# Lightning attention and a locality-gated expert layer on one core: the first expert tile turned outside TensorE, gate chances computed in earlier steps, one group of slot products, and another order of the first pair's weight transfers

## The chip, the core and the metric

The kernel runs on one core of a Trainium2 chip. The metric is device time in microseconds (us); smaller is better. One execution was also taken by the hardware profiler. The engines are named as in the profile: PE is TensorE (PEld its weight loads), DVE is VectorE, ACT is ScalarE, POOL is GpSimd, SP the engine that issues most of the DMAs.

## The reference

Attention: for 4 sequences of 768 tokens and 8 heads of 64, a decayed linear attention in blocks, with a running state per head. Its output, written as x with 512 values per token, goes to an expert layer with 8 experts:

```python
logits = np.einsum('bsd,de->bse', x, w_gate)
local_gate = 1.0 / (1.0 + np.exp(-np.einsum('bsd,de->bse', x, w_local).squeeze(-1)))
...
        fresh_e = int(np.argmax(logits[b, s]))
        if s == 0 or local_gate[b, s] < 0.5:
            e = fresh_e
        else:
            e = prev_e if prev_e >= 0 else fresh_e
        prev_e = e
...
        p /= p.sum() + 1e-09
        h = np.maximum(x[b, s] @ w1[e], 0.0)
        out[b, s] = p[e] * (h @ w2[e])
```

So each token has one expert, the fresh one or that of the token before it; a token's output is scaled by the chance p[e] of its expert.

## The kernel before, in words

**Attention.** The work is cut into 24 steps s (0 to 23), one for each 128-token chunk c (6) of each sequence b (4), in the order c outer, b inner. A step issues, on PE: the scores of step s+1 (`scores`, two PSUM tiles ps0 and ps1; steps in the list WIDE use 8 matmuls over 128 columns, L200, the others 16 smaller ones, L208), the part that comes from the state (`from_state`, L235), the part from the masked scores (`mix`, L248), the state update (`update`, L262; not in the last chunk) and four transpositions that turn rows of the step before (`rows_of`, L272). DVE masks the scores (L212, two operations) and adds the state (L265). ACT copies the attention output from the PSUM pair po0, po1 into xc (L251), the turned rows from pk1 into xn (L277), and decays the state (L239). po0, po1 and pk1 exist once, so the next step's L235 and L272 wait until these copies are done. POOL prepares qd and kd (L177, L180), three buffers each. xn goes to the DRAM tensor x_dram: ACT's queue issues these DMAs, in the last steps SP's.

**Routing beside attention.** After every four steps, `gates` and `logits` compute the gate logits of four row tiles of 128 tokens (there are 24). A table `extras` places the routing work at points (s, 0), in the middle of step s, and (s, 1), at its end. For the first 12 row tiles (PARTS 0 and 1) it finds experts (`fresh_experts`, `along_sequences`, `experts_of`), ranks (`ranks`), tiles and slots (`first_tiles`, `tokens_to_first_tiles`), and the chances (`chances`). `brought` multiplies a hit mask by five columns of `parts`: two for the token's number, three for its chance, split into three bf16 pieces. `masks` makes one-hot rows (`lane`), and `by_slots` multiplies both on PE (L619): this gives, for each slot of an expert tile, the token to gather (gidx) and its gate.

**Experts.** Five tiles of 128 tokens (KA = 5) come from the first 12 row tiles. A tile's rows are gathered from x_dram by an indirect DMA on POOL (`collect`, called by `ahead`), must be turned (features on the partitions), then `hidden` (L731) and `output` (L737) run on PE. Tile 0 is turned on PE by `first_turned` (L712) with one DVE copy (L713). All others are turned by `flipped`, a DVE transposition that works inside 32x32 blocks (L717), and `moved`, which puts the blocks in place by sixteen small ACT copies (L724, four for each k). After the five single tiles follow pairs of tiles of one expert (`pair`), computed with seven products for eight (L957, L962) from sums and differences of weights (`sums_1`, `sums_2`, on DVE, L935 to L938). Beside the first pairs run tiles of half size for what remains of an expert (`hooks_of_halves`: L1086, L1096, L1118).

**Weights.** There are three weight buffers (w1t and w2t, 0 to 2), 2 MB for each layer. `weights_of(g, i, layers)` issues the load of tile g's expert into buffer i on SP's queue. SP works through its queue in order and waits, at each load, until the buffer is free. G2 is the number of the first half-size tile; its weights go to buffer 2, whose first-layer half is also the room of `val` in the second `brought`.

**Order.** PE, DVE, SP and POOL run in the written order in the attention and single-tile phase. ACT is not in that list there: a scheduler places ACT's instructions. In the pair phase (from L1180) ACT is in written order as well, and POOL is not.

```python
    with tc.manual_schedule(engines={PE, DVE, SP, POOL}):
```

Of the kernel before, what the change touches and what calls it, by code (L numbers as in the profile page):

```python
# [38 lines left out]
PARTS = [(0, 8), (8, NA), (NA, NT)]  # L39
LOADS = 6  # L40
QUARTERS = [16, 17, 18, 19]
WIDE = [3, 4, 5, 6]
WARM = 10
KA = -(-(NA * P - E * (P - 1)) // P)

# [19 lines left out]
def kernel(  # L65
# [313 lines left out]
    def hot_of(i):  # L379
        lo, hi = PARTS[i]  # L380
        return hots[lo // NA][:, :, lo % NA:lo % NA + hi - lo]
# [81 lines left out]
        nc.vector.tensor_tensor(lane, countb.unsqueeze(1).broadcast_to([P, hi - lo, P]),  # L463
                                place[:, 0, lo:hi].unsqueeze(2).broadcast_to([P, hi - lo, P]), ALU.is_equal)

    def chances(i):

        lo, hi = PARTS[i]
        n = hi - lo
        if i == 2:  # L470
            room = act.tile([P, DM], F32, name="room", bufs=1)
        else:
            room = att.tile([P, DM], F32, name="kd", bufs=3)
        prob = room[:, :n * E].rearrange("p (n e) -> p n e", e=E)
        den, pick = (room[:, k:k + n] for k in (n * E, n * (E + 1)))
        nc.vector.tensor_tensor(prob, lt[:, lo:hi, :E], nows["mx", i].unsqueeze(2).broadcast_to([P, n, E]), ALU.subtract)
        nc.scalar.activation(prob, prob, ACT.Exp)
        nc.vector.tensor_reduce(den, prob, axis=AX.X, op=ALU.add)
        nc.vector.tensor_scalar(den, den, 1e-9, None, ALU.add)
        nc.vector.reciprocal(den, den)  # L480
        nc.vector.tensor_tensor(prob, prob, hot_of(i).rearrange("p e t -> p t e"), ALU.mult)
        nc.vector.tensor_reduce(pick, prob, axis=AX.X, op=ALU.add)
        nc.vector.tensor_tensor(pick, pick, den, ALU.mult)
        for k in range(2, 5):
            nc.vector.tensor_copy(parts[:, lo:hi, k], pick)
            if k < 4:
                nc.vector.tensor_tensor(pick, pick, parts[:, lo:hi, k], ALU.subtract)

    def span(i):
        return ((0, KA), (KA, G))[i]  # L490
# [216 lines left out]
    def ahead(g, i):  # L707
        collect(xgt[i], *at(g))

    def first_turned():  # L710
        for d in range(DT):
            nc.tensor.transpose(pr[:, P * d:P * d + P], xgt[0][:, P * d:P * d + P], ident)  # L712
        nc.vector.tensor_copy(xtt[0].rearrange("p d i -> p (d i)"), pr)  # L713

    def flipped(xq, xg):

        nc.vector.transpose(xq, xg)  # L717
# [48 lines left out]
    def number(k, n):  # L766
# [4 lines left out]
    extras = {  # L771
        (6, 1): constants_2, (7, 1): constants_3, (8, 1): constants_4, (9, 1): constants_5, (10, 1): constants_6,
        (9, 0): lambda: fresh_experts(0), (10, 0): lambda: along_sequences(0), (11, 0): lambda: experts_of(0),
        (12, 0): lambda: ranks(0), (13, 0): lambda: fresh_experts(1), (14, 0): lambda: (along_sequences(1), masks(0)),
        (15, 0): lambda: experts_of(1), (16, 0): lambda: ranks(1), (17, 0): first_tiles,
        (18, 0): tokens_to_first_tiles, (19, 0): lambda: (brought(0, (0, 1)), masks(1)),
        (19, 1): lambda: by_slots(0, (0, 1)), (20, 0): lambda: (ahead(0, 0), ahead(1, 1), rows_out(0)),
        (20, 1): lambda: chances(0), (21, 0): lambda: chances(1), (22, 0): lambda: brought(0, (2, 3, 4)),
    }

    def extra_work(s, k):
# [3 lines left out]
    with tc.manual_schedule(engines={PE, DVE, SP, POOL}):  # L785

        warm = pg.tile([P, A, P], F32, name="pk0")
        for _ in range(WARM):
            nc.tensor.matmul(warm[:, 0], lhsT=ident, rhs=ident, start=True, stop=True)
        masks_of_lam()  # L790
        nc.gpsimd.memset(wgt, 0.0)
        constants_1()

        for s in range(LOADS - 1):
            inp[s] = load.tile([P, 4, DM], F32, name="inp")
        for s, half in ((0, 0), (1, 0), (0, 1), (1, 1), *((s, half) for s in range(2, LOADS - 1) for half in range(2))):
            nc.sync.dma_start(out=inp[s][:, 2 * half:2 * half + 2], in_=qkv[s][:, 2 * half:2 * half + 2])
        for s in range(3):
            prepare(s)
        scores(0)  # L800
        nc.sync.dma_start(out=wgt[:, :, :E + 1], in_=wg)
        for s in range(NS):
            if s + LOADS - 1 < NS:
                loaded(s + LOADS - 1)
            if s + 3 < NS and s != 1:
                prepare(s + 3)
            if s in QUARTERS:
                j = QUARTERS.index(s)
                nc.sync.dma_start(out=w1t[0][:, j], in_=w1_src(0)[:, j])
            if s == NS - 4:  # L810
                nc.sync.dma_start(out=w2t[0], in_=w2_src(0))
                weights(0)
            if s == NS - 1:
# [12 lines left out]
            mix(s)  # L826
            if s == 0:
                update(0)
                query_powers(0)
            if s in (1, 2, 3, 4):  # L830
                scores(s + 1)
            if s == 1:
                query_powers(1)
                prepare(4)
                rows_of(0)
            if s:
                update(s)
            if s + 1 == NS:
                first_turned()
            if s > 1:  # L840
                rows_of(s - 1)
            extra_work(s, 1)
        x_ctx.close()
        act = ctx.enter_context(tc.tile_pool(name="act", bufs=2))
        w1t.append(act.tile([P, DT, F], F32, name="w1_2", bufs=1))
        w2t.append(act.tile([P, FT, DM], F32, name="w2_2", bufs=1))
        pools.append(act)

        pys.extend(pg.tile([P, DM], F32, name=f"pk{i}") for i in range(2))
        hq.update({(f, 1): act.tile([P, FT // 2, P], F32, name=f"h{f}1", bufs=1) for f in range(2)})  # L850
        xgh = act.tile([P, DM], F32, name="xgh", bufs=1)
        yt = act.tile([P, 2, DM], F32, name="y", bufs=1)
        xps = [act.tile([P, DT, P], F32, name=f"xp{i}", bufs=1) for i in range(3)]
        xs = act.tile([P, 3, DT // 2, P], F32, name="xs", bufs=1)
        s1 = act.tile([P, 3, DT // 2, F // 2], F32, name="s1", bufs=1)
        yl = s1[:, 0]
        s2 = act.tile([P, 3, FT // 2, DM // 2], F32, name="s2", bufs=1)
        hs = act.tile([P, 4, FT // 2, P], F32, name="hsum", bufs=1)
        part = act.tile([P, 3, FT // 2, P], F32, name="part", bufs=1)
        rest = act.tile([P, DM // 2], F32, name="rest", bufs=1)  # L860

        def finished(g):
            output(g % 2, g % 2)
            written(g, g % 2)

        def hiddens(g):
            hidden(g % 2, g % 2, 0)
            hidden(g % 2, g % 2, 1)


        xqs.extend((xlast, rt.tile([P, DM], F32, name="lg")))
        ahead(2, 0)
        xq = hq[1, 0].rearrange("p f i -> p (f i)")
        flipped(xq, xgt[1])
        ahead(3, 1)
        moved(xtt[1], xq, (0, 1))
        hidden(0, 0, 0)
        rows_of(NS - 1)
        weights(1)
        gates(NC - 1)  # L880
        moved(xtt[1], xq, (2, 3))
        hidden(0, 0, 1)
        by_slots(0, (2, 3, 4))
        logits(NC - 1)
        fresh_experts(2)
        flipped(xqs[1], xgt[0])
        ahead(4, 0)
        moved(xtt[0], xqs[1])
        finished(0)
        weights(2)  # L890
        along_sequences(2)
        flipped(xqs[0], xgt[1])
        hiddens(1)
        moved(xtt[1], xqs[0])
        experts_of(2)
        chances(2)
        flipped(xqs[1], xgt[0])
        finished(1)
        weights(3)
        ranks(2)  # L900
        masks(2)
        other_tiles()
        tokens_to_other_tiles()
        hiddens(2)
        moved(xtt[0], xqs[1])
        output(0, 0)
        weights(4)
        brought(1, (0, 1, 2, 3, 4))
        written(2, 0)
        hiddens(3)  # L910
        weights_of(KA, w_of(0), (1,))
        output(1, 1, range(FT // 2))
        by_slots(1, (0, 1, 2, 3, 4))
        weights_of(G2, 2)
        output(1, 1, range(FT // 2, FT))
        written(3, 1)

# [262 lines left out]
    with tc.manual_schedule(engines={PE, DVE, SP, ACTE}):  # L1180
        more, fulls, halves = (number(k, n) for k, n in enumerate((PMAX - PMIN + 1, E + 1, FIRST_SMALL + 1)))
        weights_of(KA, w_of(0), (2,))
        both_halves()
        pair_ahead(0)
        rows_out(1)
# [147 lines left out]
```

## Time and profile before

| | |
|---|---|
| time, median of 3 runs | 453.33 us (451.4 to 454.59) |
| profiled execution, its own time | 451.95 us |
| its span | 450.1 us, granted TensorE clock 0.994 |
| PE busy | 431.8 us (96%) |
| DVE, ACT, POOL busy | 278.9 us (62%), 201.7 us (45%), 109.3 us (24%) |
| DMA | 124.85 MB, mean 277 GB/s |
| 32x128 block copies on ACT (L724) | 295 ns each |

The profiled execution's time is its span and some 2 us around it. In lines of the profile, `L731 PE MATMUL ps<-xt,w` means: line 731 of the kernel, on PE, a matmul into ps from xt and w. A square bracket after an instruction holds the idle time of its engine just before it and what ended it. In a table of waits the numbers are the total in us, how many times, and the longest. The attention phase reaches to about 102 us, the single tiles to 178 us, the pairs and half-size tiles from there on.

### The profile page before, as it was taken

The page shows a single profiled execution, that of the slowest core. Times are in us where ns is not written, and L with a number is a line of the kernel's source. Part 1 is how long each engine was busy: PE and PEld are TensorE (multiplying, and loading weights), DVE is VectorE, ACT ScalarE, POOL GpSimd, SP SyncE. Part 2 cuts the span into 40 slices and gives each one's busy share as a digit, 9 for nine tenths or more (in the row PEclk, how much of TensorE's full clock was granted, in tenths as well). Part 3 has the DMA queues.
Part 4 walks back from the last instruction along what each step waited for, and adds up shares of the span by engine and source line. Part 5 has one row for each costly group of instructions (what it writes and reads, how often), then busy time and mean ns, then how long its engine had stood idle before and what let it go on. Part 6 is the DMA issues. An engine that isn't in the chain of part 4 may idle for free.

```text
span 450.1 us, 10497 instructions
## 1 busy us (share of the span) xinstructions
PE 431.8 (96%) x4186; PEld 358.5 (80%) x4186; DVE 278.9 (62%) x562; ACT 201.7 (45%) x594; POOL 109.3 (24%) x120
## 2 busy tenths in 40 slices
PE   6999998899999999799999999999999999999993
PEld 5877786778667776788685999677799999898982
DVE  5547776871429949576463796100487888878661
ACT  2356665547454104543524448441445455556110
POOL 4476565231100041203220400110102011020101
PEclk9999999999999999999999999999999999999997
DMA  8999999979899899999994499997163838380101
GB/s 269 409 420 411 327 305 317 360 260 367 310 375 353 287 400 379 358 387 399 388 345 176 145 404 375 352 348 286 43 211 93 309 103 284 147 280 6 52 3 51
DMA packets 42575, 124.85 MB, mean 277 GB/s; under 512 B 3148, under 2 KB 3148, under 8 KB 40592
## 3 DMA queue, kind: packets, MB, share of 16 engines
q1 hardware_dynamic: 34976, 104.62, 63.4%
q0 software_dynamic: 4368, 13.90, 9.0%
q10 hardware_dynamic: 3168, 5.51, 3.2%
q8 instruction: 37, 0.61, 0.5%
q14 instruction: 26, 0.21, 0.1%
HBM read 124.02 MB, written 12.91 MB: 304 GB/s over the span
## 4 chain that ended last, share of the span: by engine, by line
PE 77%; DMA 12%; issue 6%; DVE 4%; POOLq 0%; POOL 0%
PE ps L731 11%; PE pk L962 11%; PE pk L737 11%; PE ps L957 10%; DMA out_dram<-y,sidxp 6%; PE po L248 5%; DMA w<-in_w_dram 5%; PE po L957 5%; PE pl L962 4%; PE ps L208 3%; PE pk L272 3%; PE pk L262 2%; PE po L235 2%; PE pr L1118 2%; PE pr L1096 2%
## 5 line engine op out<-in xcount | busy, mean ns | idle before, releaser
L731 PEld LDWEIGHTS ps<-xt,w 128*128 128x128 f32 x512 | 58.2, 192 | 3.0 <-issue 2.3
L731 PE MATMUL ps<-xt,w 128*128 128x128 f32 x512 | 59.1, 276 | 0.3 <-DVE xt L713 0.3
L737 PE MATMUL pk<-w,h 128*128 128x512 f32 x128 | 56.5, 593 | 0.0
L737 PEld LDWEIGHTS pk<-w,h 128*128 128x128 f32 x128 | 23.6, 190 | 26.3 <-issue 25.6
L703 POOL DMA_INDIRECT xg<-x_dram,gidx x25 | 25.8, 1032 | 59.2 <-DVE lg L717 27.7
L746 POOL DMA_INDIRECT out_dram<-y,sidx x14 | 14.0, 1001 | 105.8 <-DVE y L763 46.5
L212 DVE TENSOR_TENSOR sm<-ps,mask 128x512 f32<-128x512 f32 x46 | 29.7, 685 | 15.1 <-PE ps L208 7.6
L724 ACT COPY xp<-xlast 32x128 f32<-32x128 f32 x128 | 37.8, 295 | 1.7
L733 ACT ACTIVATE h<-ps 128x512 f32<-128x512 f32 x16 | 9.6, 597 | 57.6 <-PE ps L731 57.6
L724 ACT COPY xp<-lg 32x128 f32<-32x128 f32 x112 | 33.0, 295 | 2.6
L763 DVE TENSOR_SCALAR y<-pk,gate 128x512 f32<-128x512 f32 x8 | 5.9, 743 | 42.1 <-PE pk L737 30.4
L957 PEld LDWEIGHTS ps<-xp,w 128*128 128x128 f32 x256 | 30.5, 192 | 1.7 <-issue 1.3
L177 POOL TENSOR_TENSOR qd<-inp,lamq 128x512 f32<-128x512 f32 x20 | 25.6, 1278 | 24.9 <-PE po L235 11.4
L957 PE MATMUL ps<-xp,w 128*128 128x128 f32 x256 | 31.3, 275 | 0.0
L957 PE MATMUL ps<-xs,s 128*128 128x128 f32 x256 | 31.2, 275 | 0.0
L962 PE MATMUL pk<-w,h 128*128 128x256 f32 x128 | 30.5, 381 | 0.0
L962 PE MATMUL pk<-s,hsum 128*128 128x256 f32 x128 | 30.3, 380 | 0.0
L248 PE MATMUL po<-sm,inp 128*64 128x128 f32 x384 | 27.7, 280 | 2.5 <-DVE sm L212 1.6
L957 PEld LDWEIGHTS ps<-xs,s 128*128 128x128 f32 x256 | 29.9, 192 | 0.0
L248 PEld LDWEIGHTS po<-sm,inp 128*64 128x64 f32 x384 | 20.9, 136 | 9.5 <-issue 6.6
L962 PEld LDWEIGHTS pk<-s,hsum 128*128 128x128 f32 x128 | 23.9, 190 | 3.3 <-DVE s L1045 0.2
L962 PEld LDWEIGHTS pk<-w,h 128*128 128x128 f32 x128 | 23.5, 190 | 3.4 <-issue 0.6
(280 smaller groups left out, 792.0 us busy)
## 6 DMA issues: line engine op xcount, KB each, us to landing
w<-in_w_dram SPq DMA_DIRECT2D x43, 2048.0 KB, 11.4
inp<-in_qkv_dram SPq DMA_DIRECT2D x15, 1024.0 KB, 8.0
x_dram<-xn ACTq DMA_DIRECT2D x21, 256.0 KB, 7.2
inp<-in_qkv_dram SPq DMA_DIRECT2D x10, 512.0 KB, 7.7
inp<-in_qkv_dram SPq DMA_DIRECT2D x4, 768.0 KB, 6.3
w<-in_w_dram SPq DMA_DIRECT2D x4, 512.0 KB, 9.8
x_dram<-xn SPq DMA_DIRECT2D x2, 256.0 KB, 8.1
xg<-x_dram,gidx POOLq DMA_INDIRECT x25, 6.8
```

Of the source, the lines that this page charges most:

```text
L177: nc.gpsimd.tensor_tensor(qd, x[:, 0].rearrange("p (a i) -> p a i", i=P), lamq, ALU.mult)
L208: nc.tensor.matmul(ps[u][half, a, first:], lhsT=kt[rows, a, half], rhs=qt[rows, a, first:], start=True, stop=True, skip_group_check=True)
L212: nc.vector.tensor_tensor(sm[:, u], ps[u], mask[:, u], ALU.mult)
L248: nc.tensor.matmul(head(a, u), lhsT=vn[:, a, u], rhs=sm[:, u, a], start=(not c and a < 2), stop=True, skip_group_check=True)
L272: nc.tensor.transpose(px[:, P * a:P * a + P], xc[:, a, ORDER[s][0]], ident)
L703: nc.gpsimd.indirect_dma_start(out=xg, out_offset=None, in_=x_dram[:n, :], in_offset=bass.IndirectOffsetOnAxis(ap=gidx[i][:, j:j + 1], axi ...
L724: copy(xt[QP * j:QP * j + QP, :, QP * k:QP * k + QP], blocks[QP * k:QP * k + QP, :, j])
L731: nc.tensor.matmul(ph[:, j], lhsT=w1t[w][:, d, P * f:P * f + P], rhs=xtt[i][:, d], start=(d == 0), stop=(d == DT - 1))
L737: nc.tensor.matmul(pys[i], lhsT=hq[f // 4, i][:, f % 4], rhs=w2t[w][:, f], start=(f == 0), stop=(f == FT - 1))
L746: apart(nc.gpsimd.indirect_dma_start(out=out, out_offset=bass.IndirectOffsetOnAxis(ap=sidx[i][:, j:j + 1], axis=0), in_=y, in_offset=None, ...
L957: nc.tensor.matmul(to[:, m], lhsT=a[:, k, P * m:P * m + P], rhs=b[:, k], start=(new and not m and not k), stop=(k == 1), skip_group_check= ...
L962: nc.tensor.matmul(to, lhsT=a[:, f], rhs=b[:, f], start=(new and not f), stop=(f == FT // 2 - 1), skip_group_check=True)
```

## The change

It has five parts.

1. Step 6 leaves WIDE: its scores use the 16 smaller matmuls.
2. `chances` for PARTS 0 and 1 is split into three pieces and moved from (20, 1) and (21, 0) to the ends of steps 11, 12, 13 and 15, 16, 17. Its room is h10 (the tile `hq[1, 0]`, not otherwise used so early) instead of a kd buffer.
3. `brought` and `by_slots` for the first tiles handle all five columns at once, at (19, 0) and (19, 1). Before, columns 0 and 1 were handled there, and columns 2 to 4 at (22, 0) and, on PE, after the second half of tile 0's `hidden`.
4. `first_turned` is gone. Tile 0 is turned as the others are: `flipped` at (21, 1) into xlast, then `moved` in four parts at (21, 1), (22, 0), (22, 1) and (23, 0). The gather of tile 2 is issued right after that `flipped`. xlast takes the last step's turned rows afterwards, as before.
5. `weights_of(G2, 2)`, the weights of the first half-size tile, is issued after the first pair's second-layer weights on SP's queue instead of before them. (The first pair's first-layer weights stay where they are, ahead of both.)

```diff
-WIDE = [3, 4, 5, 6]
+WIDE = [3, 4, 5]
...
-    def chances(i):
+    def chances(i, ks=range(3)):
...
-            room = att.tile([P, DM], F32, name="kd", bufs=3)
+            room = hq[1, 0].rearrange("p f i -> p (f i)")
...
-    def first_turned():
-        for d in range(DT):
-            nc.tensor.transpose(pr[:, P * d:P * d + P], xgt[0][:, P * d:P * d + P], ident)
-        nc.vector.tensor_copy(xtt[0].rearrange("p d i -> p (d i)"), pr)
-
...
-        (12, 0): lambda: ranks(0), (13, 0): lambda: fresh_experts(1), (14, 0): lambda: (along_sequences(1), masks(0)),
-        (15, 0): lambda: experts_of(1), (16, 0): lambda: ranks(1), (17, 0): first_tiles,
-        (18, 0): tokens_to_first_tiles, (19, 0): lambda: (brought(0, (0, 1)), masks(1)),
-        (19, 1): lambda: by_slots(0, (0, 1)), (20, 0): lambda: (ahead(0, 0), ahead(1, 1), rows_out(0)),
-        (20, 1): lambda: chances(0), (21, 0): lambda: chances(1), (22, 0): lambda: brought(0, (2, 3, 4)),
+        (11, 1): lambda: chances(0, (0,)), (12, 0): lambda: ranks(0), (12, 1): lambda: chances(0, (1,)), (13, 0): lambda: fresh_experts(1), (13, 1): lambda: chances(0, (2,)), (14, 0): lambda: (along_sequences(1), masks(0)),
+        (15, 0): lambda: experts_of(1), (15, 1): lambda: chances(1, (0,)), (16, 0): lambda: ranks(1),
+        (16, 1): lambda: chances(1, (1,)), (17, 0): first_tiles, (17, 1): lambda: chances(1, (2,)),
+        (18, 0): tokens_to_first_tiles, (19, 0): lambda: (brought(0, (0, 1, 2, 3, 4)), masks(1)),
+        (19, 1): lambda: by_slots(0, (0, 1, 2, 3, 4)), (20, 0): lambda: (ahead(0, 0), ahead(1, 1), rows_out(0)),
+        (21, 1): lambda: (flipped(xlast, xgt[0]), ahead(2, 0), moved(xtt[0], xlast, (0,))),
+        (22, 0): lambda: moved(xtt[0], xlast, (1,)), (22, 1): lambda: moved(xtt[0], xlast, (2,)),
+        (23, 0): lambda: moved(xtt[0], xlast, (3,)),
...
-            if s + 1 == NS:
-                first_turned()
...
-        ahead(2, 0)
...
-        by_slots(0, (2, 3, 4))
...
-        weights_of(G2, 2)
         output(1, 1, range(FT // 2, FT))
...
         weights_of(KA, w_of(0), (2,))
+        weights_of(G2, 2)
         both_halves()
```

More of the change, by code (lines that the diff above doesn't have):

```diff
@@ L472, in chances @@
         else:
-            room = att.tile([P, DM], F32, name="kd", bufs=3)
+            room = hq[1, 0].rearrange("p f i -> p (f i)")
         prob = room[:, :n * E].rearrange("p (n e) -> p n e", e=E)
         den, pick = (room[:, k:k + n] for k in (n * E, n * (E + 1)))
[L476 to L487, printed above, removed]
+        if 0 in ks:
+            nc.vector.tensor_tensor(prob, lt[:, lo:hi, :E], nows["mx", i].unsqueeze(2).broadcast_to([P, n, E]), ALU.subtract)
+            nc.scalar.activation(prob, prob, ACT.Exp)
+        if 1 in ks:
+            nc.vector.tensor_reduce(den, prob, axis=AX.X, op=ALU.add)
+            nc.vector.tensor_scalar(den, den, 1e-9, None, ALU.add)
+            nc.vector.reciprocal(den, den)
+            nc.vector.tensor_tensor(prob, prob, hot_of(i).rearrange("p e t -> p t e"), ALU.mult)
+            nc.vector.tensor_reduce(pick, prob, axis=AX.X, op=ALU.add)
+            nc.vector.tensor_tensor(pick, pick, den, ALU.mult)
+        if 2 in ks:
+            for k in range(2, 5):
+                nc.vector.tensor_copy(parts[:, lo:hi, k], pick)
+                if k < 4:
+                    nc.vector.tensor_tensor(pick, pick, parts[:, lo:hi, k], ALU.subtract)
     def span(i):
```

## The prediction

> **What bounds the kernel now.** I read the page's busy table first, then TensorE's waits, then the chain of waits and the timeline in the two stretches that the change touches. The page:
>
> ```profile
> PE 431.8 (96%) x4186; PEld 358.5 (80%) x4186; DVE 278.9 (62%) x562; ACT 201.7 (45%) x594; POOL 109.3 (24%) x120
> ```
>
> TensorE is busy for 431.8 of 450.1 us. Nothing gains unless it takes TensorE work away or closes one of its few gaps. Its waits by releaser:
>
> ```profile
> PE po L957 <- DVE part L1004: 2.9, 1, 2.9
> PE pk L789 <- POOL ident masks.py:199: 2.0, 1, 2.0
> ...
> PE po L235 <- issue: 1.4, 1, 1.4
> PE ps L208 <- issue: 1.2, 1, 1.2
> ...
> PE ps L731 <- DVE xt L713: 0.3, 1, 0.3
> ```
>
> Two are within the change's reach: 2.9 us in the first pair and 0.3 us ahead of the first expert tile. The chain of waits shows where the first begins:
>
> ```profile
> 164.55 21.52 DMA w<-in_w_dram
> 186.09 1.24 DVE s L937
> 187.35 1.23 DVE w L937
> ...
> 189.20 0.58 DVE part L1003
> 189.81 0.70 DVE part L1004
> 190.54 2.05 PE po L957 x16
> ```
>
> The second-layer weights of the first pair are issued at 164.55 and land 21.5 us later. VectorE's sums (L937) wait for them, and L1004 behind them frees the PSUM bank that the next product needs. TensorE stands from 187.60 to 190.54. The attention's end, from the timeline:
>
> ```profile
> 91.64 1.21 POOL L703 DMA_INDIRECT xg<-x_dram,gidx  x1 [0.16 <-DVE got L641]
> ...
> 96.96 0.59 ACT L277 COPY xn<-pk 128x512 f32<-128x512 f32 x1
> ...
> 99.04 0.65 ACT L251 COPY xc<-po 128x256 f32<-128x256 f32 x2 [1.50 <-PE po L248]
> ...
> 99.73 0.67 PE L235 MATMUL po<-qd,kv 64*64 64x128 f32 x16
> ...
> 102.05 0.69 DVE L713 COPY xt<-pr 128x512 f32<-128x512 f32 x1 [1.82 <-PE pr L712]
> ...
> 102.79 3.84 PE L731 MATMUL ps<-xt,w 128*128 128x128 f32 x32 [0.34 <-DVE xt L713]
> ...
> 103.39 4.90 ACT L724 COPY xt<-h 32x128 f32<-32x128 f32 x16 [0.32 <-DVE h L717]
> ```
>
> The reader is to see three things. The first gather starts at 91.64, and the view of that one DMA gives 6.0 us to landing: 97.7. ScalarE is nearly empty between steps. Turning a tile off TensorE costs ScalarE sixteen copies in 4.90 us, 0.306 each, after a VectorE transposition of 0.70 (L717).
>
> **What the Trainium skill says.** "VectorE: DVE Perf Modes", The three transpose paths: VectorE transposes only 32x32 blocks. This is why the other tiles need sixteen block copies; the trace agrees (0.70 and then 4.90 us). "Perfetto Trace Analysis", Matmuls: independent groups should rotate through PSUM banks so that one is emptied while the next is filled. The pair "po" does not rotate: the next step's L235 writes the banks that L251 empties; in the trace L235 starts at 99.73, as the copies end at 99.69. "DMA: Bandwidth & Descriptors", Queues, rings and completion order: on each DMA engine a row's descriptors are consumed in ring order. The trace agrees: weights issued at 161.77 took 18.4 us (landing 180.2), those of 164.55 landed after them at 186.1. "SBUF — State Buffer", Who interferes with whom: a VectorE operation with two SBUF inputs contends with a GpSimd one that reads SBUF. The trace agrees: two "val" products took 1.31 us beside a GpSimd product (86.36 to 87.64), and 0.16 each without one at 99.75.
>
> **The change, part by part.** Against the profiled execution: span 450.1, time 451.95, which lies 1.4 below the median 453.33 of the runs shown.
>
> Step 6 not wide. The wide form (L200) takes 1.09 us in the chain, the split form (L208) 0.81. TensorE is back to back there: -0.28.
>
> Chances moved to steps 11 to 17. The same VectorE instructions as at 91.63 to 94.71: for eight tiles 0.27, then six in 1.45, then five in 1.0. Up to step 15 they fit: VectorE has two tiles of scores to mask (1.29) and one state update (0.42) in a step of 3.4 us; at step 12, the fullest, it still sits idle 0.99 us, and a mask ready 0.5 late is not due for another 3 us. ScalarE's two exponentials (0.26) find their input ready. From step 16 VectorE runs without slack: at 76.94 its idle time before the mask is 1.01 us, and 1.35 of new work goes in; at 80.87 it is 0.26 and 1.0 goes in. So the mask of step 19 ends about 0.8 later than now and the next scores, which need its PSUM, start about 0.05 late. Step 18's 2.3 us of slot work and step 19's "hit" follow it without a gap.
>
> All five slot products together. Three more "val" products, 3 x 0.16 = 0.5 us, directly ahead of the "lane" mask (0.68) that the slot matmuls wait for. Now "lane" ends at 88.46 and the matmuls at 88.77; afterwards about 89.05 and 89.35. Net shift after step 19, with the 0.28 already in it: +0.5. TensorE's "issue" gap of 1.2 us at 84.1 sits inside this stretch; if it goes, VectorE is still the later one. The second group of twelve slot matmuls (111.56 to 111.95) disappears: -0.4 there.
>
> First expert tile off TensorE. Removed: four transposes (0.60), the copy L713 and the wait of 0.34. Added: one transposition on VectorE and sixteen copies on ScalarE, and here I followed the built order of ScalarE's queue. In it stand, after step 21's xc copies: one block copy (waits for the transposition), xn, one block copy, the x_dram issue, nine block copies, and only then xc of step 22, one block copy, xn, four block copies. The gather is issued behind the last qd on GpSimd, which waits for step 20's L235, so it shifts with TensorE: landing 97.7 + 0.5 = 98.2, transposition to 98.9. ScalarE until xc of step 22 is done: 11 x 0.306 + 0.59 + about 0.16 for the DMA issue + 0.65 = 4.8, so 103.7 instead of 99.7. TensorE's L235 of step 23 waits for those banks. Behind it are queued L248, the four transposes L272, and L731, and the whole expert phase behind them. From 103.8: 0.60 + 1.02 + 0.55 = 106.0 for L731; the last block copies end at 105.85. Against 102.79 this is +3.2. The slot group saved makes it +2.8 when the first output starts. GpSimd's later gathers are earlier, which nobody needs; SP's x_dram write waits for the late xn, and the weights of tile 1 behind it go out some 4 us later: landing about 114.5 and 120.5 for a use at 122.6 and 130, hidden.
>
> First pair's weights first. Issued at the same point of TensorE's work (end of L737), but now the first transfer pending. The first-layer weights, with little ahead, took 8.0 us (155.65 to 163.6), so I expect 8 to 9.5, done well before L937 wants them 18.5 us after the issue. L937 then starts at 183.15 in today's frame, the two sums end at 185.65, the transposition at 186.35, L1003 and L1004 at 187.75, and TensorE, free at 187.60, waits 0.25: -2.7. What is late next: the two half-tile weights leave 3.4 to 4 us later, and the DMA engines stand idle for about 2.7 us (163.6 to 166.3), while the share of the stretch 163 to 236 is 1.0. So everything behind arrives about 2.7 us later, while TensorE is 2.7 earlier: 5.4. The tightest I find: weights issued at 218.9 landed at 230.0 and were used at 236.13 (L1096), slack 6.1. It holds, barely.
>
> Sum: +2.8 - 2.7 = +0.1 on 451.95, so 452.05 in the profiled frame, and 453.4 beside the median.
>
> **Rivals.** A: the block copies do not hold TensorE. For it: TensorE waited for ScalarE nowhere. Then L731 starts 0.60 + 0.34 + 0.28 earlier, less 0.5 + 0.3 for the late slots, and the slot group and the pair gain are kept: -0.4 - 0.4 - 2.7 = -3.5, and at the best, with no slot delay, -4.3: 449.8 to 449.0, I take 449.4. Against it: the copies cannot start before the landing, and 6.9 us of ScalarE work then stands ahead of L731.
>
> B, slower: the DMA backlog takes the pair gain back. If the queue behind runs more than 0.7 us later than I found, the half-tile product L1096, or L1118 at 223, waits instead of L957. Each further us costs one; with 2 to 3 us of it the time is 453.4 + 2.7 = 456.1. For it: share 1.0 up to 236. Against: slack in every case that I priced.
>
> C, slower: the gather lands later. Each us after 98.2 moves the transposition, ScalarE and L731 by one. The gathers on this tile took up to 6.8 us, so 0.8 more; with VectorE's slot work 1 us worse as well (five "val" at 0.65 instead of 0.16): +1.8, 455.2.
>
> **How the numbers follow.** Forecast 0.55, A 0.22, B and C together 0.23. The forecast's own range: ScalarE's block 0.8 either way, slots 0.5, TensorE's unexplained "issue" gaps (1.4, 1.2 and 0.5 us now, which may move or go) 1.4; together about 1.9: 451.5 to 455.3. With A's and B's values the range is 449.4 to 456.8. About 1% is what a measurement of this kernel can tell from no change, 4.5 us. A reaches this only if an "issue" gap goes as well, B only with C: faster 0.14, same 0.75, slower 0.11.
>
> **What would show it.** Right: TensorE's waits list L235 behind ScalarE's xc for 3 to 4 us near 100; the block copies begin near 98.9; L731 starts near 106; the L957 wait is 0.5 us or less, with the weights landing within 10 us; no new wait at L1096 or L1118. Wrong: L731 starts before 103 (A), a DMA wait in the first two pairs (B), or a slot matmul that waits over 1 us for VectorE.

## The result, and the profile after

The changed kernel takes 453.09 us, median of 20 runs (449.15 to 455.77); the kernel before, in the same rounds, 453.04 us (448.88 to 457.67). The ratio, which like all ratios here is taken over fast runs alone (those within 1.5% of a kernel's fastest) and need not be that of the medians, is 1.0028, 95% interval 1.0004 to 1.0052; the ratio of these medians is 1.0001. It is at most a trace slower. The profiled execution took 452.62 us with a span of 450.8 us and a granted clock of 0.993.

The page's busy table and the clock's row of the changed kernel:

```profile
PE 433.8 (96%) x4186; PEld 360.3 (80%) x4186; DVE 278.9 (62%) x561; ACT 206.6 (46%) x610; POOL 109.4 (24%) x120
...
PEclk9999999998999999999999999999999999999998
```

TensorE is busy 2.0 us longer than before, though four transpositions left it. The one 8 inside the clock row, in the tenth slice, is the first sign of why. TensorE's waits by releaser (total, times, longest):

```profile
PE po L235 <- ACT xc L251: 2.8, 1, 2.8
PE pk L790 <- POOL ident masks.py:199: 2.0, 1, 2.0
...
PE ps L208 <- issue: 0.8, 1, 0.8
PE po L248 <- DVE sm L212: 0.6, 2, 0.4
PE pr L622 <- DVE val L612: 0.3, 1, 0.3
```

The pair's wait of 2.9 us is gone and one of 2.8 us stands at L235 behind ScalarE's xc. The table has no entry for L1092 or L1114, the half-size tiles' products. Lines moved a little: `flipped` is now L715, `moved` L722, `hidden` L729, `output` L735, the pair's first product L953. The timeline at the attention's end:

```profile
93.11 1.21 POOL L706 DMA_INDIRECT xg<-x_dram,gidx  x1 [0.17 <-issue]
...
98.05 0.71 DVE L715 STREAM_TRANSPOSE xlast<-xg 128x512 f32<-128x512 f32 x1 [1.52 <-DMA xg<-x_dram,gidx]
...
98.80 0.30 ACT L722 COPY xt<-xlast 32x128 f32<-32x128 f32 x1 [1.31 <-DVE xlast L715]
...
99.97 2.75 ACT L722 COPY xt<-xlast 32x128 f32<-32x128 f32 x9
...
102.75 0.65 ACT L251 COPY xc<-po 128x256 f32<-128x256 f32 x2
...
103.26 1.30 PE L235 MATMUL po<-qd,kv 64*64 64x128 f32 x16 [2.78 <-ACT xc L251]
...
104.49 1.97 PE L248 MATMUL po<-sm,inp 128*64 128x128 f32 x16
...
106.39 0.77 PE L272 MATMUL pk<-ident,xc 128*128 128x128 f32 x4
```

The gather landed at 98.03; the transposition, eleven block copies on ScalarE and then xc at 102.75 followed: the chain of the prediction. New are the durations after it. L235 takes 1.30 us instead of 0.67, L248 1.97 instead of 1.09. Busy times by stretch (from, to, length, busy of PE, PEld, DVE, ACT and POOL, then PEclk, DMA share, GB/s):

```profile
100.50:103.30 2.80, 0.04 (x2) 0.07 (x3) 0.05 (x1) 2.69 (x10) 0.99 (x1) 0.99 0.79 229
103.30:107.20 3.90, 3.90 (x38) 3.24 (x39) 0.00 (x0) 3.68 (x12) 0.00 (x0) 0.57 0.59 144
107.20:110.80 3.60, 3.60 (x35) 3.60 (x34) 0.00 (x0) 3.47 (x11) 0.00 (x0) 1.00 0.96 382
```

TensorE stands still for 2.8 us, and for the next stretch the granted clock is about half. The clock record of this execution has it as one stretch of 3.413 us at 0.5, from 103.26 on. The first pair, in the timeline of the kernel before:

```profile
186.09 1.22 DVE L937 TENSOR_TENSOR s<-w 128x1024 f32<-128x1024 f32 x1 [2.97 <-DMA w<-in_w_dram]
...
190.54 2.05 PE L957 MATMUL po<-xs,w 128*128 128x128 f32 x16 [2.95 <-DVE part L1004]
```

and in that of the changed one:

```profile
168.31 0.37 SPq L690 DMA_DIRECT2D w<-in_w_dram  x1
...
186.80 1.21 DVE L933 TENSOR_TENSOR s<-w 128x1024 f32<-128x1024 f32 x1
...
190.50 0.69 DVE L1000 TENSOR_TENSOR part<-part,po 128x512 f32<-128x512 f32 x1
...
191.24 1.94 PE L953 MATMUL po<-xs,w 128*128 128x128 f32 x15
```

The sum L933 (L937 before) waits for no DMA any more, and the product behind L1000 has no wait either.

### The profile page after: what moved, and what is told of

Read it like the earlier page. It is cut to its first block, busy times and chain, and to the rows that moved or that the text cites. A ratio compares the mean times of both kernels' runs of the same rounds, so it can differ in the third digit from the quotient of the medians.

```text
span 450.8 us, 10511 instructions
## 1 busy us (share of the span) xinstructions
PE 433.8 (96%) x4186; PEld 360.3 (80%) x4186; DVE 278.9 (62%) x561; ACT 206.6 (46%) x610; POOL 109.4 (24%) x120
## 4 chain that ended last, share of the span: by engine, by line
PE 78%; DMA 11%; issue 6%; DVE 2%; ACT 1%; POOLq 0%; POOL 0%; SPq 0%; ACTq 0%
PE ps L729 13%; PE pk L735 12%; PE ps L953 12%; PE pk L958 11%; DMA out_dram<-y,sidxp 6%; PE po L953 5%; PE po L248 5%; PE pl L958 4%; PE ps L208 3%; DMA w<-in_w_dram 2%; PE pk L272 2%; PE pk L262 2%; PE pr L1114 2%; PE pr L1092 2%; PE po L235 2%
## 5 line engine op out<-in xcount | busy, mean ns | idle before, releaser
L729 PEld LDWEIGHTS ps<-xt,w 128*128 128x128 f32 x512 | 58.2, 192 | 2.4 <-issue 2.3
L729 PE MATMUL ps<-xt,w 128*128 128x128 f32 x512 | 59.0, 276 | 0.0
L735 PE MATMUL pk<-w,h 128*128 128x512 f32 x128 | 56.5, 593 | 0.0
L735 PEld LDWEIGHTS pk<-w,h 128*128 128x128 f32 x128 | 23.6, 190 | 26.3 <-issue 25.6
L722 ACT COPY xp<-xlast 32x128 f32<-32x128 f32 x128 | 37.8, 295 | 1.7
L731 ACT ACTIVATE h<-ps 128x512 f32<-128x512 f32 x16 | 9.6, 597 | 58.2 <-PE ps L729 58.2
L722 ACT COPY xp<-lg 32x128 f32<-32x128 f32 x112 | 33.0, 295 | 2.6
L953 PEld LDWEIGHTS ps<-xp,w 128*128 128x128 f32 x256 | 30.5, 192 | 1.7 <-issue 1.3
L953 PE MATMUL ps<-xp,w 128*128 128x128 f32 x256 | 31.3, 275 | 0.0
L953 PE MATMUL ps<-xs,s 128*128 128x128 f32 x256 | 31.2, 275 | 0.0
L248 PE MATMUL po<-sm,inp 128*64 128x128 f32 x384 | 28.7, 286 | 1.7 <-issue 1.2
L953 PEld LDWEIGHTS ps<-xs,s 128*128 128x128 f32 x256 | 29.9, 192 | 0.0
L248 PEld LDWEIGHTS po<-sm,inp 128*64 128x64 f32 x384 | 21.9, 140 | 9.3 <-issue 7.6
```

The costliest lines, as they stand in the source:

```text
L248: nc.tensor.matmul(head(a, u), lhsT=vn[:, a, u], rhs=sm[:, u, a], start=(not c and a < 2), stop=True, skip_group_check=True)
L722: copy(xt[QP * j:QP * j + QP, :, QP * k:QP * k + QP], blocks[QP * k:QP * k + QP, :, j])
L729: nc.tensor.matmul(ph[:, j], lhsT=w1t[w][:, d, P * f:P * f + P], rhs=xtt[i][:, d], start=(d == 0), stop=(d == DT - 1))
L731: nc.scalar.activation(hq[half, i], ph, ACT.Relu)
L735: nc.tensor.matmul(pys[i], lhsT=hq[f // 4, i][:, f % 4], rhs=w2t[w][:, f], start=(f == 0), stop=(f == FT - 1))
L953: nc.tensor.matmul(to[:, m], lhsT=a[:, k, P * m:P * m + P], rhs=b[:, k], start=(new and not m and not k), stop=(k == 1), skip_group_check= ...
```

## The experiments

Twelve kernels; a ratio is always to the kernel before on the same chip, and 1% is 4.5 us. The first four undo or apply two of the five parts.

**Part 5 alone** (the kernel before with the new order of the pair's weights):

```diff
-        weights_of(G2, 2)
         output(1, 1, range(FT // 2, FT))
...
         weights_of(KA, w_of(0), (2,))
+        weights_of(G2, 2)
```

> Part 5 alone on the kernel before. If the order of the weights is what removes the wait of 2.95 us in the first pair, and the half-size tiles' weights stay in time behind it: TensorE's wait at L957 is 0.3 us or less, no wait for a DMA appears at the half-size tiles, and the time is 2.7 to 3.0 us (0.6 to 0.65%) below the kernel before. If the backlog takes the gain back (rival B of the prediction), a wait of 1 us or more stands at L1096 or L1118 and the time is within 1 us of the kernel before.

Measured: 448.68 us (8 runs), ratio 0.9905, interval 0.9874 to 0.9936. No product of the pairs is left in TensorE's waits. The gain, 4.3 us (2.9 to 5.7), is larger than was expected and than the 2.95 us that were waited. It is the shortest time of all kernels here, though from eight runs alone.

**Part 4 alone** (the first tile turned off TensorE in the kernel before, its chances and slots as they were):

```diff
-        (20, 1): lambda: chances(0), (21, 0): lambda: chances(1), (22, 0): lambda: brought(0, (2, 3, 4)),
+        (20, 1): lambda: chances(0), (21, 0): lambda: chances(1), (22, 0): lambda: (brought(0, (2, 3, 4)), moved(xtt[0], xlast, (1,))),
+        (21, 1): lambda: (flipped(xlast, xgt[0]), ahead(2, 0), moved(xtt[0], xlast, (0,))),
+        (22, 1): lambda: moved(xtt[0], xlast, (2,)), (23, 0): lambda: moved(xtt[0], xlast, (3,)),
...
-                first_turned()
```

> Part 4 alone on the kernel before: the first tile is turned by VectorE and sixteen ScalarE copies; chances, slot products, WIDE and weights are as before. If the copies hold the PSUM pair and so TensorE: a wait of L235 of step 23 for ScalarE's xc of some 3 us, followed by a stretch of half TensorE clock in this execution, L731 at 106 to 108 instead of 102.8, and a time 3 to 5 us above the kernel before. If instead the slot work on VectorE (parts 2 and 3) is what delays the changed kernel's attention end, this kernel has no such wait and its time is 0.5 to 1 us below the kernel before (0.60 of transpositions and 0.34 of wait saved).

Measured: 456.61 us, ratio 1.0081 (1.0052 to 1.0109): +3.7 us. Its waits of TensorE:

```profile
PE po L951 <- DVE part L998: 2.9, 1, 2.9
PE po L235 <- ACT xc L251: 2.5, 1, 2.5
```

and the stretches around both:

```profile
98.00:100.50 2.50, 0.02 (x1) 0.01 (x1) 1.50 (x5) 2.43 (x9) 1.32 (x2) 0.98 0.39 103
100.50:104.20 3.70, 3.68 (x36) 3.04 (x37) 0.00 (x0) 3.52 (x12) 0.28 (x1) 0.55 0.60 160
188.90:191.83 2.93, 0.01 (x1) 0.00 (x0) 2.90 (x5) 0.00 (x0) 1.01 (x1) 1.00 0.99 396
191.83:195.30 3.47, 3.47 (x19) 3.47 (x20) 2.60 (x3) 1.12 (x2) 0.00 (x0) 0.61 0.98 355
```

It has both holes, and after each the clock column falls from about 1 to near 0.6.

**Part 4 undone** (the changed kernel with `first_turned` back):

```diff
+            if s + 1 == NS:
+                first_turned()
...
-        (21, 1): lambda: (flipped(xlast, xgt[0]), ahead(2, 0), moved(xtt[0], xlast, (0,))),
-        (22, 0): lambda: moved(xtt[0], xlast, (1,)), (22, 1): lambda: moved(xtt[0], xlast, (2,)),
-        (23, 0): lambda: moved(xtt[0], xlast, (3,)),
```

> The changed kernel with part 4 undone: the first tile is turned on TensorE again, the rest is kept. If the copies on ScalarE cost 4.4 us at the attention's end, this kernel loses the wait of 2.8 us and the slow clock after it, keeps the gain in the first pair, and lies 3.5 to 4.2 us below the changed kernel and about 3 us below the kernel before. If the slot work is to blame, it lies within 1 us of the changed kernel.

Measured: 451.0 us, ratio 0.9958 (0.9933 to 0.9982). Against the changed kernel's 1.0028 the tile costs 0.70%, 3.2 us, a little under the 3.5 to 4.2 expected; the kernel is 1.9 us faster than the one before, where about 3 was expected.

**Part 5 undone** (the changed kernel with the old order of weights):

```diff
+        weights_of(G2, 2)
         output(1, 1, range(FT // 2, FT))
...
         weights_of(KA, w_of(0), (2,))
-        weights_of(G2, 2)
```

> The changed kernel with part 5 undone. If the two parts add up, the wait of about 2.9 us at L957 is back, and the time is 2.7 to 3.0 us above the changed kernel, 3 to 4 us above the kernel before. If the later TensorE of this kernel already gives the weights the time that they need, the wait is gone without part 5 and the time equals the changed kernel's.

Measured: 458.36 us, ratio 1.0080 (1.0041 to 1.0119). Both waits are there, 3.1 and 2.3 us:

```profile
PE po L954 <- DVE part L1001: 3.1, 1, 3.1
PE po L235 <- ACT xc L251: 2.3, 1, 2.3
```

By the ratios the new order gains 0.52%, 2.4 us, inside the changed kernel. The runs of this kernel spread from 452.11 to 462.66 us, and the ratio of the medians is 1.0120: by the medians the gain is 5.4 us. The expected 2.7 to 3.0 lie between; the size is not fixed better than that.

**Parts 4 and 5 undone**, so that only step 6's form, the earlier chances and the one group of slots are left (the diffs of the two experiments before, together):

> The changed kernel with the first tile turned on TensorE again and the old order of the first pair's weights: only the form of step 6's scores, the earlier chances and the one group of slot products are left. Prediction's sum for these: -0.28, +0.5 in front of the tiles in all, -0.4 for the second slot group, so +0.1 us: ratio 1.000. Rival (one group of slots delays the gather, as all five products stand ahead of it, and with it the first tile): first L729 over 1 us later than at 102.79, ratio 1.002 to 1.004. Third: the group saved and the earlier chances free VectorE beside the first tile, ratio 0.997 to 0.998.

Measured: 453.64 us, ratio 1.0019 (0.9994 to 1.0045): +0.9 us, between the first two expectations; a gain is next to excluded. The first tile's `hidden` started at 101.65 in its trace, not late. The executions differ by this much: the part-5 kernel has the same program as the kernel before up to there, and starts `hidden` at 101.08 against 102.79. In its execution the "issue" gaps of 1.41 and 1.24 us near 71 and 84 are absent, and shorter ones of 0.7 and 0.8 us stand elsewhere.

**Parts 3 and 4 undone** (slots in two groups, tile on TensorE; chances, step 6 and the new weight order kept):

```diff
-        (18, 0): tokens_to_first_tiles, (19, 0): lambda: (brought(0, (0, 1, 2, 3, 4)), masks(1)),
-        (19, 1): lambda: by_slots(0, (0, 1, 2, 3, 4)), (20, 0): lambda: (ahead(0, 0), ahead(1, 1), rows_out(0)),
...
+        (18, 0): tokens_to_first_tiles, (19, 0): lambda: (brought(0, (0, 1)), masks(1)),
+        (19, 1): lambda: by_slots(0, (0, 1)), (20, 0): lambda: (ahead(0, 0), ahead(1, 1), rows_out(0)), (22, 0): lambda: brought(0, (2, 3, 4)),
...
+        by_slots(0, (2, 3, 4))
```

> The first tile turned on TensorE and the slot products in two groups as before, with the earlier chances, step 6 not wide, and the new order of the first pair's weights: the changed kernel without parts 3 and 4. It differs from the run with the tile turned on TensorE (0.9958) only in the slot products, and from the order alone (0.9905) only in the chances and step 6. Theory (the prediction: one group of slots costs 0.5 us and saves 0.4, the earlier chances cost nothing): 0.990 to 0.992 if the order's 4.3 us hold. Rival one (the chances between steps 11 and 17 delay the attention): 0.994 to 0.996. Rival two (the order alone was measured too well with its 8 executions): all of these near 0.994.

Measured: 449.80 us, ratio 0.9940 (0.9917 to 0.9964). It lies in the first rival's band, close to the second's value, and its interval overlaps that of part 5 alone. A second reading comes from the traces. The last slot product ends at 88.77, 86.83, 87.37 and 86.82 us in the four kernels that share the old program up to there (mean 87.45), and between 87.42 and 89.94 (mean 88.7) in the nine that share the changed one; this kernel, with the chances moved but the slots in two groups, ended it at 88.81. So parts 1 to 3 cost some 1.3 us up to this point, with a standard error of 0.5, and this one trace points to the chances or step 6 rather than the slots. The traces of the steps before tell more; they follow under "Parts 1 to 3" below.

**The gap at L235 filled** with eighteen, then with nine unused matmuls on TensorE:

```diff
+            if s + 1 == NS:
+                for _ in range(9):
+                    nc.tensor.matmul(pr[:, :P], lhsT=ident, rhs=ident, start=True, stop=True, skip_group_check=True)
             from_state(s)
```

> The changed kernel with 18 matmuls of 128x128 on ident (results unused) put on TensorE in step 23 just ahead of L235, so that the 2.8 us in which TensorE stood idle there are filled; nothing else waits for them but the bank pr. Theory (the idle gap brings the half-clock stretch of 3.4 us, in which L235, L248 and L272 took 3.90 us instead of 2.21): the granted clock stays at 1.0 in 102 to 107 us, L729 starts 1 to 1.7 us earlier than at 107.16, the ratio to the kernel before falls from 1.003 to about 0.999. Rival (these three are slow for another reason, such as the copies beside them, and the low clock is a record only): L729 stays at 107.2 or comes later, ratio 1.003 or more.

> The changed kernel with 9 matmuls of 128x128 on ident (results unused, into the bank pr) on TensorE in step 23 ahead of L235. Eighteen took 4.18 us, more than the gap of 2.78; nine take about 2.1 and end before xc lets L235 start. Theory (a wait of 2 to 3 us brings, in a share of the executions, a stretch of 3.41 us at half clock, worth about 1.7 us): L235 starts when it did, mean clock rises from 0.9925 to 0.995 or more, and the ratio falls from 1.003 to about 1.000. Rival (the clock in the records follows the load and costs nothing by itself, or other stretches bring the low clock): mean clock and ratio as in the changed kernel, 1.002 to 1.004.

Measured: eighteen 454.58 us, ratio 1.0049 (1.0027 to 1.0071); nine 453.87 us, 1.0025 (1.0005 to 1.0045). The clock did what the theory said: its mean over the runs rose from 0.9925 to 0.9949 and 0.9953, and neither profiled run has a half-clock stretch there. The time did not follow. The timeline with nine, for which the trace has eighteen records, shows that the test was not a clean one:

```profile
100.42 2.17 PE L821 MATMUL pr<-ident 128*128 128x128 f32 x18
...
103.58 0.84 PE L235 MATMUL po<-qd,kv 64*64 64x128 f32 x16 [0.99 <-ACT xc L251]
104.35 1.09 PE L248 MATMUL po<-sm,inp 128*64 128x128 f32 x16
105.37 0.66 PE L272 MATMUL pk<-ident,xc 128*128 128x128 f32 x4
105.94 3.84 PE L729 MATMUL ps<-xt,w 128*128 128x128 f32 x32
111.42 0.66 PE L272 MATMUL pk<-ident,xc 128*128 128x128 f32 x4 [1.64 <-ACT xn L277]
```

L235, L248 and L272 are at full speed again, and `hidden` starts at 105.94 instead of 107.00. But a new wait of 1.64 us stands at the next L272. ScalarE's order is a scheduler's there, and the filler changed it: thirteen copies of tile 1 now precede the last step's xc, where the changed kernel has three. The gain of about 1.1 us went into that wait. At this place the price of the half clock stays unproven.

**The pair's wait filled** in the kernel before, where ScalarE is in written order and keeps it:

```diff
         hook(4)
+        if p == 0:
+            for _ in range(9):
+                nc.tensor.matmul(pr[:, :P], lhsT=ident, rhs=ident, start=True, stop=True, skip_group_check=True)
         product_1(c, a1(p, 1, 1), xs[:, 2])
```

> The kernel before with the same nine matmuls in the first pair, ahead of the product that waits 2.95 us for L1004; the wait itself stays. Theory (that wait costs more than its length, by half-clock stretches in a share of the executions; so the new order of weights alone gained 4.3 us instead of 2.95): mean clock rises from 0.992 to about 0.995, the ratio is 0.996 to 0.998 although TensorE has 2.1 us more to do. Rival (the larger gain of the order alone has another source, such as the DMA queue): ratio 0.999 to 1.002, clock unchanged.

Measured: 450.68 us (22 runs), ratio 0.9966 (0.9944 to 0.9987), mean clock 0.9957 against 0.9914 for the kernel before in the same rounds. The timeline:

```profile
186.07 2.17 PE L1013 MATMUL pr<-ident 128*128 128x128 f32 x18
...
187.70 0.69 DVE L1004 TENSOR_TENSOR part<-part,po 128x512 f32<-128x512 f32 x1
...
188.44 2.05 PE L957 MATMUL po<-xs,w 128*128 128x128 f32 x16 [0.20 <-DVE part L1004]
```

The product still starts after L1004, and TensorE does 2.17 us of useless work more (again eighteen records for nine matmuls). The kernel is 0.34% faster all the same, 1.5 us (0.6 to 2.5). So the wait costs more than its own length, and the surplus goes when TensorE is kept busy. A stretch of 3.41 us at half clock loses 1.7 us and takes 0.0038 off a mean over 450 us; the clock rose by 0.0043, about one stretch per execution.

**The gathers ahead of the last qd** in the changed kernel:

```diff
-        (19, 1): lambda: by_slots(0, (0, 1, 2, 3, 4)), (20, 0): lambda: (ahead(0, 0), ahead(1, 1), rows_out(0)),
+        (19, 1): lambda: (by_slots(0, (0, 1, 2, 3, 4)), ahead(0, 0), ahead(1, 1)), (20, 0): lambda: rows_out(0),
```

> The changed kernel with the first two gathers issued on GpSimd right after the slot numbers are there, ahead of the last qd, instead of behind it; ScalarE's order is the same. Theory (the wait of L235 is the landing of the gather plus eleven block copies ahead of xc): the gather is issued near 90 instead of 93.1 and lands near 95 instead of 98.0; the wait of L235 falls from 2.8 us to 0 to 1.5, and the ratio by 0.003 to 0.006 against the changed kernel: 0.997 to 1.000. Rival (the landing does not decide, ScalarE's queue does: the copies wait for something else, or qd of step 23, now behind two gathers of about 1.2 us on GpSimd, comes late and holds L235 in its turn): wait of 2 us or more at L235, by GpSimd or ScalarE, ratio 1.002 or more.

Measured: 452.68 us, ratio 0.9992 (0.9971 to 1.0013), 1.6 us better than the changed kernel. The ratio is where the theory put it, the wait is not: L235 still waits 2.4 us.

```profile
88.68 1.21 POOL L706 DMA_INDIRECT xg<-x_dram,gidx  x1 [2.70 <-DVE gate L639]
...
96.30 0.71 DVE L715 STREAM_TRANSPOSE xlast<-xg 128x512 f32<-128x512 f32 x1 [1.10 <-DMA xg<-x_dram,gidx]
...
101.51 1.16 PE L235 MATMUL po<-qd,kv 64*64 64x128 f32 x16 [2.37 <-ACT xc L251]
```

The gather was issued at 88.68, but the transposition, released by it, began at 96.30: 7.6 us instead of 4.9. Most of the head start was lost in the transfer.

**The block copies shared between ScalarE and VectorE**, with the early gathers and the transposition half a step earlier:

```diff
+        (19, 1): lambda: (by_slots(0, (0, 1, 2, 3, 4)), ahead(0, 0), ahead(1, 1)), (20, 0): lambda: rows_out(0),
+        (21, 0): lambda: (flipped(xlast, xgt[0]), ahead(2, 0), moved(xtt[0], xlast, (0,))),
+        (21, 1): lambda: moved(xtt[0], xlast, (1,), nc.vector.tensor_copy),
+        (22, 1): lambda: moved(xtt[0], xlast, (2, 3), nc.vector.tensor_copy),
```

> As the early gather, and the sixteen block copies divided: four on ScalarE, twelve on VectorE, which stands idle there after step 22; the transposition is half a step earlier. Theory (nothing but the block copies on ScalarE holds TensorE in front of the expert tiles): no wait of L235 over 0.5 us, no half-clock stretch, L729 near 102.3 to 103.0, and with the pair's wait gone a ratio of 0.990 to 0.993. Rival (VectorE, behind the transposition and twelve copies, is late with the masks of step 23's scores, or copies beside each other slow down): a wait at L248 or L729 by VectorE of over 1 us, ratio 0.996 or more.

Measured: 449.99 us, ratio 0.9933 (0.9908 to 0.9959). L235 waits 1.4 us for ScalarE, one step earlier than in the changed kernel (in step 22) and behind four copies instead of eleven; `hidden` starts at 104.12, where 102.3 to 103.0 was expected. Both expectations missed on detail: the wait shrank and did not vanish, and no wait for VectorE came.

**All sixteen on VectorE**, behind the last masks, with the same early gathers and transposition:

```diff
+        (19, 1): lambda: (by_slots(0, (0, 1, 2, 3, 4)), ahead(0, 0), ahead(1, 1)), (20, 0): lambda: rows_out(0),
+        (21, 0): lambda: (flipped(xlast, xgt[0]), ahead(2, 0)),
+        (22, 1): lambda: moved(xtt[0], xlast, range(4), nc.vector.tensor_copy),
```

> The changed kernel with the two gathers right behind the slot numbers, the transposition half a step earlier, and all sixteen block copies on VectorE behind the last masks; ScalarE has none of them. Theory (only ScalarE's copies hold TensorE): no wait of L235 over 0.4 us near 100; the copies, 16 of about 0.235 us, end near 103, so that L729 waits 0 to 0.6 us for VectorE; ratio 0.989 to 0.992. Rival (the half-step of VectorE is not free: the transposition or the copies come late and L729 waits 1 us or more): ratio 0.993 to 0.996.

Measured: 450.25 us, ratio 0.9939 (0.9912 to 0.9966), mean clock 0.9955. Its timeline:

```profile
98.38 0.71 DVE L715 STREAM_TRANSPOSE xlast<-xg 128x512 f32<-128x512 f32 x1 [0.73 <-DMA xg<-x_dram,gidx]
...
100.83 3.67 DVE L722 COPY xt<-xlast 32x128 f32<-32x128 f32 x16
100.84 0.65 ACT L251 COPY xc<-po 128x256 f32<-128x256 f32 x2 [1.50 <-PE po L248]
...
101.53 0.67 PE L235 MATMUL po<-qd,kv 64*64 64x128 f32 x16
...
104.56 3.84 PE L729 MATMUL ps<-xt,w 128*128 128x128 f32 x32 [0.76 <-DVE xt L722]
```

ScalarE now waits for TensorE and not the reverse; L235 has no wait. L729 waits 0.76 us for VectorE, between the two expectations, and the ratio is in the rival's band. The early gathers alone had left 2.4 us of the wait, so it is the copies' leaving ScalarE that ends it. With the hold gone this kernel is 4.0 us faster than the changed one, but no faster, within the intervals, than the one that turns the tile on TensorE (0.9958).

## Why the prediction was right

It said 453.4 us and no measurable difference, from two large terms that cancel: the tile +2.8, the pair -2.7. The runs show both. Each part was measured in three surroundings, once against the kernel before and twice as a difference of two ratios (part 4: 0.0081, 1.0028 - 0.9958, 1.0080 - 1.0019; part 5: -0.0095, 0.9958 - 1.0019, 1.0028 - 1.0080; parts 1 to 3: 0.0019, 0.9958 - 0.9905, 1.0080 - 1.0081), at 4.53 us for 0.01 and uncertain by 1.2 to 2.2 us each:

| | predicted | measured |
|---|---|---|
| parts 1 to 3 | +0.1 (0.5 in front, -0.4 behind) | +0.9, +2.4, 0.0 |
| part 4, the tile | +2.7 (L731 at +3.2, of which slots 0.5) | +3.7, +3.2, +2.8 |
| part 5, the pair | -2.7 | -4.3, -2.8, -2.4 |
| sum | +0.1 | means +1.1 +3.2 -3.1 = +1.2; whole change +1.3 (0.2 to 2.4) |

That the sum meets the whole is no proof of it, since the whole change's own ratio stands in two of the differences. With the medians in place of the ratios, the entries that rest on the changed kernel or on the one with part 5 undone move by 1.2 to 3.0 us.

**The tile, mechanism right.** The gather landed at 98.03 (98.2 predicted), the transposition was done at 98.76 (98.9), eleven copies, xn and the DMA issue in ScalarE's queue, L235 at 103.26 (103.8). Reading ScalarE's built order, instead of assuming it idle, was the step that carried the forecast; rival A needed L729 before 103 and falls, as does C with the gather's landing. Moving the copies to VectorE removes the wait, where the early gathers alone left 2.4 us of it; so ScalarE's queue was the holder.

**The tile, size missed.** L729 starts at 107.00 where the sum had 106.0. From L235 on the sum took the durations of before, 2.17 us to L729; they were 3.74, and the 1.6 us more are what a stretch of 3.413 us at half clock would cost (1.7). The prediction treated a wait on TensorE as costing its length and nothing more. The Trainium skill, "TensorE: Matmul & The Clock Gate", Part 1: The HAM clock gate, What's actually happening, states that after an idle window of about 3.4 us the clock falls to half, that the window is 4096 cycles or 3413 ns, and that it runs free, so that the effect varies between runs. The trace agrees on the length, 3.413 us, and on the variation: the kernel before has no such stretch in its profiled run, and a mean clock of 0.9914 over 70. It does not agree that a whole idle window is needed: waits of 2.78, 2.50 and 3.13 us were enough here. What decided between waits of this size was where they fell; the last section has the figures.

**The pair, size missed in the same term.** The wait of 2.95 us vanished entirely, where 0.25 was to be left. By the filler's 1.5 us it was worth about 4.4 (3.5 to 5.5), and part 5 alone gained 4.3; with the other parts in place the ratios give 2.4 and 2.8, the medians more, so the surplus there is not established. The landing of the weights is not told by the profile for this one transfer; that they were there at 186.80 is. Rival B falls: the half-size tile's second transfer, issued behind, took 23.3 us, and no product of the first two pairs waits for a DMA. The tightest weights, with about 6 us of slack before, were issued at 219.60, landed at 234.72 and were used from 236.75 on: 2.0 us were left. The slack called "barely" enough was enough. The nearest to rival B is a DMA wait of 0.2 us at L1092 in the kernel that shares the block copies.

**Parts 1 to 3, the term that missed most.** The predicted net +0.5 at the slots' end is about +1.3 over thirteen traces. The end of each step, taken at ScalarE's last xc copy, shows where it comes from. Step 5, which issues step 6's scores, is 0.26 us shorter in all nine traces of the changed program, as predicted (0.28). But by the end of step 10, before the first moved chance has run, the nine have lost 0.7 us against the four, counted from the end of step 4, with a standard error of 0.3; the kernel with the slots apart has lost 1.0. In the written order only the form of step 6's scores differs up to there. So "Step 6 not wide ... -0.28" priced the matmuls and not what follows them: TensorE's "issue" gaps between 29 and 53 us stand at other instructions and sum to 1.1 to 2.0 us in the nine (mean 1.5), against 0.5 to 1.5 in the four (mean 0.8). Why they move is open. Steps 11 to 18, with the moved chances, add 0.8 us (standard error 0.4), steps 11 to 14 nothing (0.04, standard error 0.3); so "up to step 15 they fit" is not contradicted, and what the later pieces cost is not settled. The profiled pair of executions alone showed +0.3 at the slots' end: the execution before was the latest of its four there (88.77, the others 86.82 to 87.37).

The medians moved by +0.05 us where +0.1 was forecast, the ratio says +1.3 (0.2 to 2.4). That the two are so close is thus partly luck: all three terms were larger than predicted on the mean, and the largest two have opposite signs.

## What to carry to other kernels

When small copies are moved to an engine that looks idle, read that engine's built queue: what counts is what stands behind them there, and a scheduler may put eleven of them ahead of the one copy that TensorE needs. Price a TensorE wait of 2 us or more above its length, by up to the 1.7 us that one slow stretch costs, and test it by filling it with useless work: if the kernel gets faster, the surplus is real. Where two parts of a change cancel, run each alone; here the one edit of a DMA order (0.9905) beats the whole change, and no repair of it that was run measured lower, though the intervals of the best ones (0.9933, 0.9939, 0.9940) overlap its own. And price a changed instruction mix by more than its matmuls: a step made 0.26 us shorter was followed, on the mean, by 1.0 us of loss in the next five.

## What was not expected of the hardware

- Whether a wait is followed by the half clock depends, in these traces, on where it falls. Between the first and the last change of the clock, every stretch at full or half clock is a whole multiple of 3.413 us (28, 1 and 100 of them in the changed kernel, 129 in the kernel before). So the clock changes on a grid of that step. The grid's place differs: its first change comes 4.8 to 7.8 us after the span's start. The waits, laid on the grid of their own execution:

| wait of TensorE | us | idle in the grid steps that it touches | half clock next |
|---|---|---|---|
| changed kernel, L235 | 2.78 | 2.78 | yes |
| gathers ahead, L235 | 2.37 | 2.37 | yes |
| part 4 alone, L235 | 2.50 | 2.39 and 0.1 | yes |
| part 4 alone, pair | 2.93 | 0.3 and 2.67 | yes |
| part 5 undone, pair | 3.13 | 0.3 and 2.83 | yes |
| part 5 undone, L235 | 2.25 | 0.6 and 1.64 | no |
| kernel before, pair | 2.95 | 1.54 and 1.41 | no |
| parts 4 and 5 undone, pair | 3.42 | 1.94 and 1.47 | no |

- In all fourteen traces a grid step with 2.26 us or more of idle TensorE was followed by a step at half clock, and none with up to 1.94 us was, with one exception: in the kernel with part 4 undone the half clock came after a step with 1.53 us. A wait that a border of the grid cuts in two can thus cost its length alone, and a shorter one that lies in one step costs up to 1.7 us more. The figures are sums of matmul records, whose ends are modelled.
- Over the changed kernel's 20 runs time falls as the mean clock rises, with a correlation of -0.72 and a slope of 1.5 us for each 0.0038 of clock, one such stretch. By the square of that correlation it goes with about half of the spread from 449 to 456 us.
- A gather of 128 rows took 4.9 us from issue to landing at 93.11 and about 7.6 at 88.68, in the kernel with the early gathers. While it was under way the DMA share was 0.95 there and 0.83 in the changed kernel.
- A 32x128 block copy took 217 ns on VectorE (sixteen in 3.67 us) and 295 ns on ScalarE.
